# One PSUM tile of four banks split into four one-bank tiles, with a new order for the first pair's cycle

## The chip, the cores and the metric

The kernel runs on one core of one Trainium2 chip. The metric is the device time of the whole program in microseconds, the median of several executions. One execution was taken with the hardware profiler; its rows are used below.

## The reference

The program is a clustered attention followed by two feed-forward blocks, all in fp32.

```python
q_assign = argmax(einsum('bhsd,hcd->bhsc', q_n, c_n))     # nearest of 16 centroids, also for k
mask = q_assign[:, :, :, None] == k_assign[:, :, None, :]
scores = where(mask, scale * q @ k.T, -1e9)
attn = softmax(scores);  x = attn @ v                       # (2, 8, 768, 64) -> (1536, 512)
h = x @ w_in;   x = (h * cos(h)) @ w_out                    # d_ff 2048
h = x @ w_in2;  out = blend(h) @ w_out2                     # 0, (h+1)^2/4 or h
```

Batch is 2, there are 8 heads, 768 positions and 64 elements per head. The weights arrive as 64-bit floats and are converted on the chip.

## The kernel before, in words

The two heads of a "pair" are worked on together; there are 8 pairs (2 batches by 4 pairs of heads). Each pair is one cycle of the attention, and after the cycles come the two feed-forward blocks, which are long rows of matmuls on TensorE (PE). Every engine takes its instructions strictly in the order in which the program issues them.

That order is written out by hand as a string of words, which `run_cycle` (line 719) reads. `BEGIN` (790) is the cycle of pair 0, `CYCLE` (793) that of pairs 1 to 5, `LATE` (796) and `LAST` (799) those of pairs 6 and 7, `END` (802) the rest. A letter is a step, a digit its part, and a prime moves it to the pair before. Cycle c does these steps:

- S0 to S11: scores of one block of 128 rows (four matmuls, lines 583 and 586, into a two-bank tile of a pool of two) and its row maximum on VectorE (DVE, 593). S0 to S5 are the first head, S6 to S11 the second.
- E0 to E11: the exponential on ScalarE (ACT, 601, with the read of its sum). A pool of two score tiles means that S(n) waits for E(n-2).
- G0 to G11: three transposes of the first head's probabilities on PE (644) into a bank that `bank3()` hands out, and a copy of the bank on ACT (646). V0 to V5: probabilities times v (651), accumulated in bank 3. X: that sum times the inverse row sums, on DVE (656).
- T6 to T11: the second head's probabilities, transposed on DVE (677). W0 to W3: 192 small matmuls (686) into all four banks, the "strips". Z: the sum of the strips (`x_sum`, 692): ACT copies partitions 64 to 127 of all four banks (696), then DVE adds partitions 0 to 63 (697).
- Q0 to Q3, D, C, m, t, n, O, H, J: the preparation of the pairs to come. Q transposes q and k (491), ACT copies the bank (497), GpSimd (POOL) splits it (499, 500); D and C are products with the centroids, there and back (510, 512, 518); m and n (527, 528, 537, 538) are DVE steps that read C's bank; O transposes the one-hot rows (545, 547); H and J are DMAs (473).
- R and B: inverse row sums (608 to 617) and their spread by DMA (625, 630). L, v, r: loads of q and k (235), v (243), v of the second head (254). w: one step of the conversion of a weight chunk (157 to 176).

All DMAs of the attention are issued by one queue, SP, in the order of the words.

The PSUM is eight banks of 512 fp32 per partition. Four belong to the score tiles. The other four are one tile, `big` (line 212). `bank3()` (215) hands out its banks 0, 1 and 2 in turn; bank 3 holds V's sum, and in the first pair's preparation (`first_pair`, 291) matmuls without use (297) that keep PE busy. The framework puts in all waits between engines: an instruction waits for earlier ones of other engines that touched the same tile, by its own record of tiles.

Of the kernel before, what the change touches and what calls it, by code (L numbers as in the profile page):

```python
# [9 lines left out]
F32 = mybir.dt.float32  # L10
# [4 lines left out]
AF = mybir.ActivationFunctionType  # L15
ALU = mybir.AluOpType
# [3 lines left out]
P = 128  # L20
# [13 lines left out]
def attention_moe_moe(  # L34
# [18 lines left out]
    nc = tc.nc  # L53
    B, H, S, D = q.shape
    C = centroids.shape[1]
    NT, DM = out.shape
    DFF = w1_in.shape[1]
    NJ = S // P
    HJ = NJ // 2
    HS = S // 2  # L60
# [147 lines left out]
    with ExitStack() as actx:  # L208
        ap = actx.enter_context(tc.tile_pool(name="apool", bufs=1))
        ps_s = []  # L210
        ps_b = actx.enter_context(tc.tile_pool(name="ps_b", bufs=1, space=PSUM))
        big = ps_b.tile([P, 4, 512], F32, name="big")
        turn_of = [0]

        def bank3():
            turn_of[0] += 1
            return big[:, turn_of[0] % 3, :HS]

        idle = ap.tile([P, HS], F32, tag="pt", bufs=PT_BUFS, name="idle").bitcast(BF16)[:, :512]
        nc.vector.memset(idle, 0.0)  # L220
# [3 lines left out]
        nat, v_of, vr_of = {}, {}, {}  # L224
# [65 lines left out]

        def first_pair():

            idle_o = big[:, 3]

            def run_idle(n):
                for _ in range(n):
# [20 lines left out]
            t = nat.pop(0)  # L317
# [19 lines left out]
            def put(dst, src):  # L337
                return nc.sync.dma_start(dst.bitcast(F32), src.bitcast(F32))

            pc = bank3()[:, :P]  # L340
            turn(0, 0)
            turn(0, 1)
# [17 lines left out]
            for hf in range(2):  # L360
                nc.scalar.activation(th[:, 1, cols(hf)], qk[1, hf], AF.Copy)
                nc.vector.tensor_tensor(tl[:, 1, cols(hf)], qk[1, hf],
                                        th[:, 1, cols(hf)].bitcast(F32), ALU.subtract)

            dt = bank3()
            cw = cn32[:, 0].rearrange("p h c -> p (h c)")
            for hf in range(2):
# [46 lines left out]
            def turn_rows(h, s, pars=(0, 1)):  # L414
                po = bank3().rearrange("p (j n) -> p j n", n=P)
                for jp in range(HJ):
                    rows = dotv[h][:, s, 2 * jp:2 * jp + 2].rearrange("p r h c -> p (r h c)")
                    rows = rows[:, pars[0] * 2 * C:(pars[-1] + 1) * 2 * C]
                    nc.tensor.transpose(po[:2 * C * len(pars), jp], rows, ident)
                return {par: po[n * 2 * C:(n + 1) * 2 * C] for n, par in enumerate(pars)}  # L420
# [227 lines left out]

        def p_v(i, kt):
            for hf in range(2):  # L650
                nc.tensor.matmul(big[hf * D:(hf + 1) * D, 3, :HS], v_of[i][:, kt],  # L651
                                 pts.pop((i, 2 * kt + hf)), start=kt == 0, stop=kt == NJ - 1)

        def x_rows(i):
            x = rb[2 * i]
            nc.vector.tensor_tensor(x, big[:, 3, :HS], x, ALU.mult)

        def x_parts(i):
            x32 = rb.pop(2 * i)
# [19 lines left out]
        def p_v_square(i, n, parts):  # L679
            t, vr = sq[i], vr_of[i]  # L680
            for cp in range(12 * n // parts, 12 * (n + 1) // parts):
                for a in range(4):
                    rows = slice(32 * a, 32 * a + 32)
                    for par in range(2):
                        kt, g = divmod(2 * cp + par, 4)
                        nc.tensor.matmul(  # L686
                            big[par * D:(par + 1) * D, a, :NJ * 32],
                            vr[rows, g, kt * D:(kt + 1) * D],
                            t[rows, 2 * cp + par].rearrange("p j r -> p (j r)"),
                            start=cp == 0, stop=cp == 11, tile_position=(32 * a, par * D))  # L690

        def x_sum(i):
            x = xpool.tile([P, S], F32, tag="xs", bufs=1, name=f"xs{i}")
            xv = x[D:].rearrange("p (j a r) -> p a j r", j=NJ, r=32)
            o = big[:, :, :NJ * 32].rearrange("p a (j r) -> p a j r", r=32)
            nc.scalar.activation(xv, o[D:], AF.Copy)
            nc.vector.tensor_tensor(xv, o[:D], xv, ALU.add)
            xs[i] = x[D:]

        def x_out(i):  # L700
# [18 lines left out]
        def run_cycle(c, order):  # L719
# [4 lines left out]
            for word in words:  # L724
# [18 lines left out]
                elif what == "G":  # L743
                    p_transpose(i, arg)
                elif what == "V":
                    p_v(i, arg)
                elif what == "X":
                    x_rows(i)
                elif what == "Y":
                    x_parts(i)  # L750
                elif what == "R":
                    inverse(2 * i + arg)
                elif what == "B":
                    spread(2 * i + arg)
                elif what == "W":
                    p_v_square(i, arg, parts)
                elif what == "Z":
                    x_sum(i)
                elif what == "z":
                    x_out(i)  # L760
# [26 lines left out]
                elif what == "w":  # L787
                    pump(arg or 1)

        BEGIN = ("L' S3 m' E3 S4 t' S5 E4 H0' n' G0 E5 R0 O' G1 G2 S6 G3 G4 J0' E6 S7 G5 r T6 V0 E7 H1' V1 G6 "  # L790
                 "G7 S8 T7 B0 Q0 J1' E8 G8 G9 Q1 V2 S9 T8 G10 G11 Q2 Q3 L S10 E9 E10 T9 V3 D S11 E11 C m V4 t "
                 "n ")
        CYCLE = ("Q0 S0 Q1 S1 H0' E0 Q2 E1 T10' O' V5' S2 Q3 S3 E2 E3 J0' D T11' X' G0 S4 E4 v' S5 W0' W1' R1' "
                 "J1' E5 R0 W2' W3' Y' L Z' S6 S7 G1 B1' G2 G3 E6 C G4 E7 V0 H1' m V1 T6 T7 G5 G6 t G7 S8 n G8 "
                 "r G9 G10 E8 S9 B0 T8 V2 E9 V3 S10 G11 S11 E10 T9 E11 z' V4 ")
# [5 lines left out]
                 "S10 G11 w S11 E10 T9 E11 z' V4 ")  # L801
        END = ("T10' V5' T11' X' R1' W0' B1' W1' W2' W3' Z' Y' z' ")
        first_pair()
        for c in range(NP):
            run_cycle(c, {0: BEGIN, 6: LATE, 7: LAST}.get(c, CYCLE))
        run_cycle(NP, END)
# [8 lines left out]
    while len(wslot) < 2:  # L815
        n = len(wslot)
# [148 lines left out]
```

## Time and profile before

| | us |
|---|---|
| median of 3 executions | 940.75 (928.43 to 942.93) |
| the profiled execution, whole | 924.13 |
| its span, first to last instruction | 922.3 |
| PE busy in the span | 808.5 (88%) |
| DVE busy | 587.6 (64%) |
| ACT busy | 365.1 (40%) |
| POOL busy | 254.4 (28%) |
| mean granted PE clock, share of full speed | 0.913 |

The times of rows are counted from the span's start. Busy time of PE counts the modelled ends of matmuls that follow one another in a pipeline, so that two neighbours overlap in the sum. In a row of the timeline, the brackets give how long the engine sat idle before the instruction and what ended the wait.

### The profile page before, as it was taken

The numbers are of one execution on the slowest core, as the hardware profiler recorded it, in microseconds if no ns is written. First come the engines' busy times: TensorE is split into PE (matmuls) and PEld (weight loads), VectorE is DVE, ScalarE is ACT, GpSimd is POOL, SyncE is SP. The second block draws the span as 40 slices with busy tenths as digits, with TensorE's granted clock in tenths as the row PEclk, the third lists the DMA queues.
The fourth block names the chain that finished last, engine by engine and source line by source line (L and its number), as shares of the span: only waits on it lengthen the run. The fifth ranks groups of instructions, "written<-read, shape, count | busy, mean of one in ns | idle before, by whom it ended". The sixth has DMA issues, their size and how long they took to land.

```text
span 922.3 us, 12700 instructions
## 1 busy us (share of the span) xinstructions
PE 808.5 (88%) x4957; PEld 619.6 (67%) x4957; DVE 587.6 (64%) x805; ACT 365.1 (40%) x650; POOL 254.4 (28%) x374
## 2 busy tenths in 40 slices
PE   7677777767777777849999999999999999999998
PEld 4445454545454544638888888888888888888887
DVE  4425453653446574688777878888888687764543
ACT  3534353563454454345443344343225433222220
POOL 5123433443242223443222212123332112211110
PEclk8659696997599788979999999999999999999999
DMA  7524635372437422222122212121121221100012
GB/s 172 133 64 93 142 68 140 71 178 72 104 93 173 105 65 53 101 91 91 57 85 90 87 50 92 47 92 45 47 92 47 92 83 54 46 1 1 0 46 92
DMA packets 52621, 74.97 MB, mean 81 GB/s; under 512 B 28977, under 2 KB 36369, under 8 KB 52561
## 3 DMA queue, kind: packets, MB, share of 16 engines
q1 hardware_dynamic: 52272, 73.99, 29.0%
q8 instruction: 39, 0.64, 0.3%
q14 instruction: 22, 0.17, 0.1%
q10 hardware_dynamic: 288, 0.16, 0.1%
HBM read 50.89 MB, written 3.19 MB: 59 GB/s over the span
## 4 chain that ended last, share of the span: by engine, by line
PE 78%; ACT 6%; DVE 6%; issue 4%; DMA 3%; POOL 2%; SPq 1%; ACTq 0%; DVEq 0%; POOLq 0%
PE y L859 9%; PE y L861 9%; PE y L860 9%; PE h L859 9%; PE h L860 9%; PE h L861 9%; PE big L644 6%; PE big L651 4%; PE s L583 3%; PE s L586 3%; PE big L686 3%; ACT p_t L646 3%; DMA st<-tt 2%; DVE nm L593 2%; SPq L473 1%
## 5 line engine op out<-in xcount | busy, mean ns | idle before, releaser
L593 DVE TENSOR_REDUCE nm<-s 128x1 f32<-128x768 f32 x96 | 90.7, 955 | 119.7 <-PE s L586 118.7
L859 PE MATMUL h<-xh,w 128*128 128x512 f32 x384 | 151.2, 394 | 15.1 <-DVE g L838 12.2
L860 PE MATMUL h<-xl,w 128*128 128x512 f32 x384 | 150.7, 393 | 0.0
L861 PE MATMUL h<-xh,w 128*128 128x512 f32 x384 | 150.6, 392 | 0.0
L821 POOL TENSOR_SCALAR gh<-g 128x512 fp32r<-128x512 f32 x96 | 73.4, 765 | 278.8 <-DVE g L852 159.8
L644 PE MATMUL big<-ident,p 128*128 128x128 f32 x288 | 65.2, 347 | 49.7 <-ACT p_t L646 29.3
L601 ACT ACTIVATE p<-s,nm 128x768 f32<-128x768 f32 x96 | 86.3, 899 | 33.9 <-DVE nm L593 31.6
L644 PEld LDWEIGHTS big<-ident,p 128*128 128x128 f32 x288 | 39.2, 171 | 81.8 <-ACT p_t L646 45.0
L859 PEld LDWEIGHTS h<-xh,w 128*128 128x128 f32 x384 | 73.0, 190 | 31.5 <-DVE g L838 12.9
L646 ACT ACTIVATE p_t<-big 128x384 f32<-128x384 f32 x96 | 47.1, 490 | 108.5 <-PE big L644 107.9
L825 DVE TENSOR_TENSOR gl<-g,gh 128x512 fp32r<-128x512 f32 x96 | 74.5, 776 | 21.8 <-POOL gh L821 15.8
L583 PE MATMUL s<-st,st 128*128 128x384 f32 x192 | 82.5, 429 | 3.7 <-ACT p L601 3.4
L848 ACT ACTIVATE p<-h,ones 128x512 f32<-128x512 f32 x48 | 33.0, 688 | 133.0 <-DVE m L847 132.6
L860 PEld LDWEIGHTS h<-xl,w 128*128 128x128 f32 x384 | 73.1, 190 | 15.4 <-issue 0.3
L861 PEld LDWEIGHTS h<-xh,w 128*128 128x128 f32 x384 | 72.8, 190 | 15.3
L157 ACT ACTIVATE wx<-wraw 128x1024 f32<-128x1024 f32 x32 | 36.1, 1129 | 104.9 <-DVE w L176 46.1
L586 PE MATMUL s<-st,st 80*128 80x384 f32 (+1 forms) x192 | 73.6, 383 | 1.9 <-DVE st L429 1.9
L859 PE MATMUL y<-gh,w 128*128 128x512 f32 x192 | 74.7, 389 | 0.0
L860 PE MATMUL y<-gl,w 128*128 128x512 f32 x192 | 74.7, 389 | 0.0
L861 PE MATMUL y<-gh,w 128*128 128x512 f32 x192 | 74.7, 389 | 0.0
L861 PE MATMUL y<-w,gl 128*128 128x512 f32 (+1 forms) x192 | 74.3, 387 | 0.0
L860 PE MATMUL y<-w,gh 128*128 128x512 f32 (+1 forms) x192 | 74.3, 387 | 0.0
(138 smaller groups left out, 1419.5 us busy)
## 6 DMA issues: line engine op xcount, KB each, us to landing
wraw<-in_moe_w_in_dram SPq DMA_DIRECT2D x16, 1024.0 KB
wraw<-in_moe_w_out_dram SPq DMA_DIRECT2D x16, 1024.0 KB
st<-tt SPq DMA_DIRECT2D x63, 192.0 KB
st<-tt SPq DMA_DIRECT2D x16, 384.0 KB
vr<-in_v_dram SPq DMA_DIRECT2D x32, 192.0 KB
nat<-in_q_dram SPq DMA_DIRECT2D x8, 384.0 KB
nat<-in_k_dram SPq DMA_DIRECT2D x8, 384.0 KB
out_dram<-acc SPq DMA_DIRECT2D x11, 256.0 KB
```

Of the source, the lines that this page charges most:

```text
L583: nc.tensor.matmul(s[:, step, :HS], qt[:, 0, cols], kt[:, 0, kc], start=True, stop=False)
L586: nc.tensor.matmul(s[:, step, :HS], qt[:rows, 1, cols], kt[:rows, 1, kc], start=False, stop=True)
L593: nc.vector.tensor_reduce(nm, s[:, :, :HS], AX.XY, ALU.max, negate=True)
L601: nc.scalar.activation(p.rearrange("p (a n) -> p a n", a=2), s[:, :, :HS], AF.Exp, bias=nm, accum_out=dens[d][:, jj:jj + 1])
L644: nc.tensor.transpose(ps[:, jj * P:(jj + 1) * P], p[:, kt * P:(kt + 1) * P], ident)
L646: nc.scalar.activation(pt, ps, AF.Copy)
L651: nc.tensor.matmul(big[hf * D:(hf + 1) * D, 3, :HS], v_of[i][:, kt], pts.pop((i, 2 * kt + hf)), start=kt == 0, stop=kt == NJ - 1)
L821: nc.gpsimd.tensor_scalar(hi, g, 1.0, 0.0, ALU.mult, ALU.add)
L825: nc.vector.tensor_tensor(lo, g, hi.bitcast(F32), ALU.subtract)
L859: nc.tensor.matmul(o, lh, rh, start=first, stop=False)
L860: nc.tensor.matmul(o, lh, rl, start=False, stop=False)
L861: nc.tensor.matmul(o, ll, rh, start=False, stop=last)
```

## The change

Four tiles of one bank each take the place of the one tile of four. Everything that used a bank of `big` uses a tile now. The turn of `bank3()` begins with bank 0 in place of bank 1. The sum of the strips is made in four steps of one bank, each an ACT copy and a DVE add of 192 columns (64 partitions), where it was one copy and one add of 768 columns. `BEGIN` holds the same words in another order: the transposes G0, G2 and G4, which need the first three blocks alone, come before the scores of the blocks after them, and Q0 to Q3 come earlier.

```diff
-        big = ps_b.tile([P, 4, 512], F32, name="big")
-        turn_of = [0]
+        big = [ps_b.tile([P, 512], F32, name=f"big{n}") for n in range(4)]
+        turn_of = [2]
 
         def bank3():
             turn_of[0] += 1
-            return big[:, turn_of[0] % 3, :HS]
+            return big[turn_of[0] % 3][:, :HS]
...
-            idle_o = big[:, 3]
+            idle_o = big[3]
...
-                nc.tensor.matmul(big[hf * D:(hf + 1) * D, 3, :HS], v_of[i][:, kt],
+                nc.tensor.matmul(big[3][hf * D:(hf + 1) * D, :HS], v_of[i][:, kt],
...
-            nc.vector.tensor_tensor(x, big[:, 3, :HS], x, ALU.mult)
+            nc.vector.tensor_tensor(x, big[3][:, :HS], x, ALU.mult)
...
-                            big[par * D:(par + 1) * D, a, :NJ * 32],
+                            big[a][par * D:(par + 1) * D, :NJ * 32],
...
             xv = x[D:].rearrange("p (j a r) -> p a j r", j=NJ, r=32)
-            o = big[:, :, :NJ * 32].rearrange("p a (j r) -> p a j r", r=32)
-            nc.scalar.activation(xv, o[D:], AF.Copy)
-            nc.vector.tensor_tensor(xv, o[:D], xv, ALU.add)
+            for a in range(4):
+                o = big[a][:, :NJ * 32].rearrange("p (j r) -> p j r", r=32)
+                nc.scalar.activation(xv[:, a], o[D:], AF.Copy)
+                nc.vector.tensor_tensor(xv[:, a], o[:D], xv[:, a], ALU.add)
...
-        BEGIN = ("L' S3 m' E3 S4 t' S5 E4 H0' n' G0 E5 R0 O' G1 G2 S6 G3 G4 J0' E6 S7 G5 r T6 V0 E7 H1' V1 G6 "
-                 "G7 S8 T7 B0 Q0 J1' E8 G8 G9 Q1 V2 S9 T8 G10 G11 Q2 Q3 L S10 E9 E10 T9 V3 D S11 E11 C m V4 t "
-                 "n ")
+        BEGIN = ("L' S3 G0 m' E3 t' G2 S4 G4 E4 n' S5 H0' E5 Q0 O' G1 Q1 G3 S6 V0 Q2 Q3 L J0' E6 G5 G6 S7 T6 V1 E7 G7 H1' G8 S8 T7 E8 G9 G10 S9 V2 T8 J1' E9 R0 r G11 D S10 V3 E10 T9 C m B0 S11 E11 V4 t n ")
```

## Rows read from the trace of the kernel before

**Rows 1.** Stretch, length, busy PE, PEld, DVE, ACT, POOL, PE clock, DMA share, GB/s.
```profile
30.10:75.00 44.90, 33.25 (x116) 20.22 (x115) 15.70 (x22) 17.38 (x36) 8.47 (x14) 0.54 0.38 90
75.00:118.80 43.80, 33.41 (x328) 21.59 (x326) 21.13 (x31) 19.54 (x40) 17.00 (x26) 0.81 0.44 102
...
202.20:252.00 49.80, 38.91 (x329) 25.64 (x327) 21.38 (x31) 20.67 (x44) 16.59 (x25) 0.69 0.40 97
252.00:291.00 39.00, 28.07 (x328) 18.83 (x326) 22.38 (x32) 20.91 (x45) 16.59 (x25) 1.00 0.54 129
291.00:331.20 40.20, 29.71 (x304) 20.50 (x305) 23.25 (x31) 19.67 (x40) 10.67 (x17) 0.83 0.51 126
331.20:372.10 40.90, 31.05 (x302) 20.86 (x304) 24.27 (x32) 18.92 (x37) 10.32 (x17) 0.79 0.21 60
372.10:405.20 33.10, 18.01 (x246) 13.93 (x242) 22.53 (x27) 9.40 (x15) 13.11 (x15) 0.81 0.21 70
405.20:922.30 517.10, 513.87 (x2268) 425.62 (x2268) 381.26 (x507) 183.74 (x287) 115.42 (x136) 1.00 0.18 62
```

**Rows 2.** Timeline of PE in the sixth cycle: start, length, instruction, idle time before it.
```profile
263.52 0.55 PE L644 MATMUL big<-ident,p 128*128 128x128 f32 x3 [2.25 <-DVE rb L656]
...
265.41 4.49 PE L686 MATMUL big<-ptb,vr 32*64 32x192 f32 x192
...
272.97 0.55 PE L644 MATMUL big<-ident,p 128*128 128x128 f32 x3 [0.58 <-ACT p_t L646]
...
278.87 0.87 PE L651 MATMUL big<-p_t,v 128*64 128x384 f32 x4 [1.33 <-DVE both L528]
...
288.88 0.49 PE L644 MATMUL big<-ident,p 128*128 128x128 f32 x3
289.13 0.42 PE L583 MATMUL s<-st,st 128*128 128x384 f32 x1
...
290.00 0.87 PE L651 MATMUL big<-p_t,v 128*64 128x384 f32 x4
```

**Rows 3.** Waits of the whole run: who waited for whom, total us, times, longest.
```profile
PE big L644 <- ACT p_t L646: 29.3, 49, 0.6
...
DVE mx L527 <- PE big L651: 23.2, 5, 5.7
...
PE big L644 <- DVE rb L656: 16.2, 7, 2.5
...
PE big L518 <- DVE st L433: 2.5, 1, 2.5
```

**Rows 4.** Timeline of ACT in the sixth cycle.
```profile
254.35 0.49 ACT L497 ACTIVATE t<-big 128x384 f32<-128x384 f32 x1 [0.70 <-POOL tt L499]
```

**Rows 5.** Groups by line: engine, instruction, count, busy us, mean ns, idle before.
```profile
L601 ACT ACTIVATE p<-s,nm 128x768 f32<-128x768 f32 x96 | 86.3, 899 | 33.9 <-DVE nm L593 31.6 <-DVE den L608 1.4
...
L646 ACT ACTIVATE p_t<-big 128x384 f32<-128x384 f32 x96 | 47.1, 490 | 108.5 <-PE big L644 107.9
...
L601 ACT ACTIVATION_READ_ACCUMULATOR p<-s,nm 128x1 f32 x96 | 18.9, 197 | 0.0
...
L697 DVE TENSOR_TENSOR xs<-big,xs 64x768 f32<-64x768 f32 x8 | 7.6, 952 | 17.8 <-ACT xs L696 17.8
...
L696 ACT ACTIVATE xs<-big 64x768 f32<-64x768 f32 x8 | 6.5, 807 | 18.9 <-PE big L686 18.8
...
L547 ACT ACTIVATE oht<-big,ohbias,ohscale 128x384 fp32r<-128x384 f32 x7 | 4.7, 666 | 1.1 <-PE big L545 1.1
L656 DVE TENSOR_TENSOR rb<-big,rb 128x384 f32<-128x384 f32 x8 | 4.3, 541 | 2.8 <-ACT both L512 2.8
```

**Rows 6.** Timeline of the SP queue in the third cycle: first and last of 12 rows.
```profile
118.13 4.55 SPq L473 DMA_DIRECT2D st<-tt  x5
...
150.27 1.11 SPq L630 DMA_DIRECT2D rb<-flat  x2
```

**Rows 7.** Busy time of the third cycle's long burst of loads, columns as in rows 1.
```profile
141.00:154.00 13.00, 8.74 (x32) 4.56 (x30) 4.07 (x6) 4.71 (x10) 5.86 (x5) 0.59 0.98 237
```

## The prediction

> **What bounds the kernel now.** I read the busy time by stretch first [rows 1]. After 405.2 us PE is busy in practically all of the 517.1 us left, at a granted clock of 1.00 (2.4 GHz): the feed-forward blocks are bound by PE's matmuls, and the change doesn't touch them. Before that lies the attention: about 30 us of preparation, BEGIN with 44.9 us, five CYCLEs with 216 us together (75.0 to 291.0), LATE and LAST with 40.2 and 40.9, and a transition of 33.1. In a CYCLE no engine is full: ACT and DVE each work 20 to 22 us of 39 to 50. So it is bound by waits between engines.
>
> The timeline of PE shows which ones [rows 2]. A group of three transposes takes PE 0.25 us when nothing stops it (288.88, next instruction 289.13). But G2 at 272.97 sat until ACT had copied the bank of the group before, though it writes another bank; G0 at 263.52 waited 2.25 us for X, a DVE read of bank 3 that G0 doesn't touch; V1 at 278.87, which writes bank 3, waited 1.33 us for DVE's step m, which reads C's bank. The list of waits [rows 3] has the same over the whole run: 29.3 us of transposes behind copies, 16.2 us behind X, and in the other direction 23.2 us of m behind V. Each of these pairs shares no bank, only the tile `big`. Whoever comes next to the tile waits for whoever came before, so three banks in turn serve as one buffer.
>
> **The cycle without these waits.** I take the sixth cycle (252.0 to 291.0), which ran at full clock. By the order string, 14 PE steps of a CYCLE wait for another bank's reader: Q1, O, V5, G0, G1, G2, G3, C, V0, V1, G6, G7, G9, G10. With a tile per bank the true waits are left: a bank is free when the copy three turns back is done, V needs its own copies, S(n) needs E(n-2). I go through the words with the durations of the rows.
>
> First part, from Q0 (251.98) to W (265.41), 13.4 us. The next late thing is ACT, which has its copies and exponentials in one order. Q1's copy starts at 254.35, 2.4 us after Q0; its wait there is for POOL [rows 4], which I leave. Behind it ACT has Q2, Q3, D and G0 to copy (with Q1 five of 0.49), O (0.67) and E0 to E3 (0.90 and 0.20 each) [rows 5]: 2.45 + 0.67 + 4.40 = 7.5. W needs G0's bank copied, so it starts at 2.4 + 7.5 = 9.9 in place of 13.4: 3.5 less. PE's own work there hides beside it: by [rows 2] a group of transposes is 0.25, an S 0.87 (289.13 to 290.00), a V 0.87, and with D taken like V that is 6 x 0.25 + 6 x 0.87 + 2 x 0.87 = 8.5.
>
> W itself, 4.4 us of PE to the next S, stays.
>
> Second part, from W's end (269.8) to the next Q0 (291.0), 21.2 us, with ten of the 14 waits. ACT has there Z, eleven copies of 0.49 and E6 to E9, before the last V4: 1.3 + 5.4 + 4.4 = 11.1. PE has six S, eleven G, C and five V: 5.2 + 3.0 + 4.4 = 12.6. Neither can start all of it at once (G1 behind Z, S10 behind E8, V2 behind G5's copy), but the S figure holds a little slack, so I take 13.0: 8.2 less. The cycle is then 39.0 - 3.5 - 8.2 = 27.3 us. ACT's whole work is 12 x 1.10 + 17 x 0.49 + 0.67 + 1.3 = 23.5, which no order can go below.
>
> **The sum of the strips.** From two rows of ACT on PSUM [rows 5], 807 ns for 768 columns and 490 for 384, one of 192 columns takes 490 - 159 = 331 ns; for DVE, 952 and 541, it is 335. Whether a copy of the second bank can run beside the add of the first, the trace doesn't show, for both write interleaved columns of one SBUF tile. If they overlap, Z takes 4 x 0.33 + 0.34 = 1.7 us, against 0.81 + 0.95 = 1.8 before; if each hands over to the other, 4 x (0.33 + 0.34) and seven handovers of 0.04 (G2's idle 0.58 holds a copy of 0.49 and two of them), 3.0. Behind it in ACT's queue stand G1's copy and E6, in DVE's the maxima of S6 and S7. G1 itself gets its bank earlier either way, after 0.7 to 2.0 us. I take 0.6 more per cycle, and in all for Z and what the two queues below may add, 29.0 in place of 27.3 us per CYCLE.
>
> The Trainium skill, Perfetto Trace Analysis, section Optimizing Scalar/DVE Operations, speaks against the split: each ScalarE or DVE instruction pays a data-access overhead, which larger operations spread. The rows agree that there is one: they give 0.17 us of an ACT copy that doesn't go with its columns, so three more copies cost 0.5 us; by the page's about 51 ns on PSUM, seen twice as long in a profile, an estimate would be 0.3. The sum changes by under 2 us over eight cycles.
>
> **What lies beside.** SP issues a CYCLE's DMAs in 23.2 us (12 rows, first and last in [rows 6]), in order; at 29 us it is 80% full. The long burst of loads runs 13 us at 237 GB/s and 0.98 of the DMA engines [rows 7]. A CYCLE moves 97 GB/s x 49.8 us = 4.8 MB, so 20 us of such a rate. Both still fit, with little room: q and k for the next Q0 are issued behind R0's DMA.
>
> **BEGIN, LATE, LAST, the preparation.** BEGIN has nine E, twelve G, four Q, O and D on ACT: 9.9 + 17 x 0.49 + 0.67 = 18.9 us. In the new order G0, G2 and G4 come before they can be held up by later scores, E8 stands before G9 and G10 (whose banks are then free without it), and R0 moves back behind E9, some 5 us before X needs it in the next cycle, enough for POOL's line and two DMAs. With the CYCLE's ratio (29.0 / 23.5) BEGIN is 23.3; it begins with PE at half clock (0.54 in [rows 1]) and loads for Q0 that are issued shortly before, so I take 27.5, 17.4 less. What the new order alone is worth can't be read; I bound it from 0 to 8 us of these. LATE and LAST have the conversion of weights on DVE: 24.3 us busy in LAST [rows 1], the most of any engine. I take 29.5 each, 22.1 less together. The preparation holds a few such waits, one of 2.5 us [rows 3]; I take 2.5, bounds 0 and 4. The transition stays: PE is busy for 18.0 of its 33.1 us and DVE for 22.5 [rows 1], the conversion of the first weights among it, none of which touches `big`.
>
> **The sum.** 2.5 + 17.4 + (216 - 5 x 29.0 = 71.0) + 22.1 = 113 us. From the profiled 924.1 that is 811. The profiled run lies 16.6 below the median shown; cycles at 0.69 and 1.00 of clock took 49.8 and 39.0 [rows 1], so the spread of the runs is probably such cycles, which a denser PE should have less of. I add 4: **815 us**.
>
> The Trainium skill, PSUM — Partial Sum Buffer, section PSUM bank collisions raise a hardware error, asks for semaphores between engines per bank and quadrant of partitions, and says that different banks run clean. The waits of [rows 3] between banks are thus more than the chip asks; if that page is right nothing else makes them come back, and the sum stands as it is.
>
> **Rivals.**
> *SP and the loads become the bound.* With ACT's waits gone, SP is 80% full, and each of its waits (for O's copy, for R's line) is idle time that it can't make up. For: [rows 6, 7]. Against: its waits lie mostly where nothing is due. Then CYCLEs are 34, LATE and LAST too, BEGIN 32: gain 2.5 + 12.9 + 46 + 13.1 = 74.5, time 850.
> *The PE clock stays low.* From [rows 1], 0.31 of clock cost 10.8 us; at 0.81, as in the second cycle, 29 becomes 35.6, BEGIN 39: gain 6 + 38 + 10 = 54, time 870. Against: two cycles with all these stalls ran at 1.00, so fewer stalls should do no worse.
> *Slower: the waits stay and Z is longer.* If the framework's record follows something other than the tile (the pool, or PSUM as a whole), the 14 waits remain and the four steps of Z hand over one by one, 1.2 us more in each of eight cycles: 924 + 10 = 934, and about 950 on the median. It decides if none of the 14 goes; one that goes (0.8 us) nearly pays for it. Against: the score tiles and those of the feed-forward blocks are separate tiles, and PE there doesn't stand behind each reader (513.9 of 517.1 us busy, [rows 1]).
>
> **Chances.** The forecast (795 to 833) 0.64, SP or loads (833 to 858) 0.22, clock (858 to 900) 0.10, waits stay 0.04. If the replay's 27.3 holds everywhere and BEGIN is 24, the gain is 127 and the time 797: the low end. The range 795 to 857 leaves out some 0.18. A measurement of this kernel tells about 2% from no change, here 19 us. Faster by more than that: 0.96; within: 0.03; slower: 0.01, the last rival at its worst.
>
> **What would show it.** Right: in the list of waits, transposes behind ACT's copies fall from 29.3 us to a few, and G behind X and m behind V vanish; CYCLEs between 27 and 31 us, with PE's clock near 1.00 and ACT over 75% busy; W some 10 us after Q0. The step is wrong where G2 and G3 still stand 1.1 us apart, where ACT sits idle behind DVE through Z, or where Q0 waits for a load. Under 795 the replay was too careful; over 857 another queue has taken over.

## The result and the profile after

The kernel after takes **781.57 us**, the median of 4 executions (779.75 to 782.67), against 936.62 of 4 of the kernel before (928.43 to 942.93): a ratio of 0.837, 95% interval 0.829 to 0.844. The direction was right. The forecast of 815 was 33 us too slow, and its range (795 to 857) lay wholly above the result.

The profiled execution took 781.32 us (span 779.5), 142.8 less than that of before. The stages first, as in [rows 1]. A cycle runs from its first Q or S on PE to the next one's.

Busy time by stretch of the kernel after: preparation, BEGIN, first, third and fourth CYCLE, LATE, LAST, transition, feed-forward blocks. Columns as in [rows 1].
```profile
0.00:18.98 18.98, 16.27 (x93) 10.00 (x95) 11.31 (x37) 11.14 (x23) 12.33 (x51) 1.00 0.87 200
18.98:42.31 23.33, 21.33 (x121) 14.22 (x118) 16.46 (x24) 16.93 (x38) 8.65 (x14) 0.93 0.76 170
42.31:70.70 28.39, 26.31 (x328) 19.23 (x326) 22.30 (x36) 19.58 (x46) 15.76 (x25) 1.00 0.72 175
97.55:123.48 25.93, 25.74 (x329) 19.26 (x327) 21.20 (x34) 20.04 (x47) 17.63 (x26) 1.00 0.82 194
123.48:148.86 25.38, 25.38 (x329) 19.14 (x327) 21.21 (x34) 20.05 (x47) 15.27 (x25) 1.00 0.76 176
175.20:202.60 27.40, 25.26 (x305) 18.44 (x304) 23.11 (x34) 19.16 (x44) 9.81 (x17) 0.94 0.74 173
202.60:229.10 26.50, 24.01 (x304) 17.37 (x304) 23.91 (x36) 18.35 (x41) 12.94 (x18) 1.00 0.40 129
229.10:262.37 33.27, 16.30 (x243) 12.76 (x241) 21.29 (x29) 9.41 (x16) 15.51 (x16) 0.85 0.22 76
262.37:779.50 517.13, 513.74 (x2268) 425.32 (x2268) 381.59 (x507) 182.96 (x287) 111.83 (x136) 1.00 0.18 62
```

Lengths in us:

| stage | before | forecast | after |
|---|---|---|---|
| preparation (to the first S of BEGIN) | 29.5 | 27.0 | 19.0 |
| BEGIN | 45.5 | 27.5 | 23.3 |
| five CYCLEs | 216 | 145 | 132.9 |
| LATE and LAST | 81.1 | 59.0 | 53.9 |
| transition and feed-forward | 550.2 | 550.2 | 550.4 |

Each stage of the attention is shorter than forecast; the last line is the same to 0.2 us. The four differences are 8, 4, 12 and 5 us; with the 4 added for the median they make the miss. (Each cycle is counted here from its first instruction on PE; the prediction took BEGIN from 30.1, 44.9 us.)

The timeline of the kernel after, in order of time: PE in the preparation, then PE, ACT and DVE in the third CYCLE (97.55 to 123.48).
```profile
9.68 1.15 PE L491 MATMUL big<-ident,nat 128*128 128x128 f32 x9
...
97.55 0.55 PE L491 MATMUL big<-ident,nat 128*128 128x128 f32 x3
...
98.74 1.01 ACT L497 ACTIVATE t<-big 128x384 f32<-128x384 f32 x2
...
103.96 0.66 PE L644 MATMUL big<-ident,p 128*128 128x128 f32 x3
...
105.54 0.49 ACT L646 ACTIVATE p_t<-big 128x384 f32<-128x384 f32 x1
...
106.22 3.95 PE L686 MATMUL big<-ptb,vr 32*64 32x192 f32 x177
110.36 0.58 PE L686 MATMUL big<-ptb,vr 32*64 32x192 f32 x15 [0.19 <-issue]
110.87 0.44 PE L583 MATMUL s<-st,st 128*128 128x384 f32 x1
...
110.99 0.98 ACT L697 ACTIVATE xs<-big 64x192 f32<-64x192 f32 x4 [2.60 <-PE big L686]
...
111.35 1.15 DVE L698 TENSOR_TENSOR xs<-big,xs 64x192 f32<-64x192 f32 x4 [2.15 <-ACT xs L697]
...
112.39 1.15 PE L644 MATMUL big<-ident,p 128*128 128x128 f32 x9
...
112.91 1.26 ACT L646 ACTIVATE p_t<-big 128x384 f32<-128x384 f32 x3 [0.94 <-PE big L644]
...
123.48 0.55 PE L491 MATMUL big<-ident,nat 128*128 128x128 f32 x3
```
Where G2 stood behind the copy of the group before [rows 2], G1, G2 and G3 now run as one piece of nine transposes in 1.15 us (112.39). G0 has no wait for X (103.96). The strips' sum takes 1.5 us (110.99 to 112.50) with copies and adds overlapping. In the 25.9 us of this cycle PE has one gap that the timeline marks: 0.19 us.

The groups of PE by line, from 97 to 202 us of the kernel after: instructions, busy us, mean ns, idle time before them.
```profile
L583 PE MATMUL s<-st,st 128*128 128x384 f32 x96 | 36.9, 384 | 1.3 <-ACT p L601 1.1
...
L644 PE MATMUL big<-ident,p 128*128 128x128 f32 x144 | 20.8, 278 | 0.8 <-ACT p L601 0.8
...
L686 PE MATMUL big<-ptb,vr 32*64 32x192 f32 x768 | 18.6, 339 | 0.6 <-issue 0.6
```
All of PE's idle time in these 105 us is 2.7. By these rows a cycle that was bound by waits is now nearly all PE's own work; as the ends of PE's matmuls are modelled, the runs below test it.

The waits of the whole run of the kernel after, columns as in [rows 3].
```profile
DVE nm L593 <- PE s L586: 16.5, 31, 3.3
PEld s L583 <- ACT p L601: 16.5, 26, 1.6
...
PE h L858 <- DVE g L837: 15.2, 2, 15.0
```
The four lines of [rows 3] are gone; DVE's maxima wait 16.5 us for scores and PE's weight loads 16.5 for exponentials, little of which stops PE in the CYCLEs (2.7 above). The longest single wait of PE is one of 15.0 us, in the transition.

### The profile page after: what moved, and what is told of

It reads as the page before. It is cut to its first block, busy times and chain, and to the rows that moved or that the text cites. A ratio compares the mean times of both kernels' runs of the same rounds, so it can differ in the third digit from the quotient of the medians.

```text
span 779.5 us, 12769 instructions
## 1 busy us (share of the span) xinstructions
PE 746.2 (96%) x4956; PEld 594.4 (76%) x4957; DVE 585.0 (75%) x829; ACT 357.5 (46%) x674; POOL 254.4 (33%) x374
## 4 chain that ended last, share of the span: by engine, by line
PE 87%; DVE 5%; POOL 2%; issue 2%; DMA 2%; ACT 1%; SPq 0%; POOLq 0%; DVEq 0%; ACTq 0%
PE y L859 11%; PE y L858 11%; PE y L860 11%; PE h L858 11%; PE h L859 10%; PE h L860 10%; PE s L583 4%; PE big L651 4%; PE big L644 4%; PE big L686 3%; PE s L586 3%; DVE nm L593 1%; PE big L491 1%; DMA wraw<-in_moe_w_out_dram 1%; ACT p L601 1%
## 5 line engine op out<-in xcount | busy, mean ns | idle before, releaser
L820 POOL TENSOR_SCALAR gh<-g 128x512 fp32r<-128x512 f32 x96 | 70.1, 730 | 280.7 <-DVE g L851 159.0
L593 DVE TENSOR_REDUCE nm<-s 128x1 f32<-128x768 f32 x96 | 90.3, 951 | 18.2 <-PE s L586 16.5
L583 PE MATMUL s<-st,st 128*128 128x384 f32 x192 | 74.0, 385 | 5.9 <-ACT p L601 4.5
L859 PE MATMUL y<-w,gh 128*128 128x512 f32 (+1 forms) x192 | 74.3, 387 | 0.0
L858 PE MATMUL y<-w,gh 128*128 128x512 f32 (+1 forms) x192 | 74.3, 387 | 0.0
L913 DVE TENSOR_TENSOR acc<-y,acc 128x512 f32<-128x512 f32 x71 | 48.3, 684 | 30.4 <-PE y L860 30.4
L173 POOL TENSOR_SCALAR w<-wx 128x1024 fp32r<-128x1024 f32 x32 | 34.6, 1082 | 102.8 <-DVE wx L167 101.0
L586 PE MATMUL s<-st,st 80*128 80x384 f32 (+1 forms) x192 | 65.7, 342 | 0.0
```

The costliest lines, as they stand in the source:

```text
L173: nc.gpsimd.tensor_scalar(hi, x, 1.0, 0.0, ALU.mult, ALU.add)
L583: nc.tensor.matmul(s[:, step, :HS], qt[:, 0, cols], kt[:, 0, kc], start=True, stop=False)
L586: nc.tensor.matmul(s[:, step, :HS], qt[:rows, 1, cols], kt[:rows, 1, kc], start=False, stop=True)
L593: nc.vector.tensor_reduce(nm, s[:, :, :HS], AX.XY, ALU.max, negate=True)
L820: nc.gpsimd.tensor_scalar(hi, g, 1.0, 0.0, ALU.mult, ALU.add)
L858: nc.tensor.matmul(o, lh, rh, start=first, stop=False)
```

## The experiments

Each kernel was timed beside the kernel before on its own chip. Ratios are to that.

**Which part of the change does it?** The kernel after with the BEGIN of before:
```diff
-        BEGIN = ("L' S3 G0 m' E3 t' G2 S4 G4 E4 n' ...
+        BEGIN = ("L' S3 m' E3 S4 t' S5 E4 H0' n' G0 ...
```


> Four one-bank tiles, with the old order of the first pair's cycle. Theory (the waits between banks carry the gain, the new order 0 to 8 us of it): 782 to 790 us, the first cycle 23 to 31 us long. Rival (the new order carries the 22 us that the first cycle lost): the first cycle stays near 40 us and the whole is at 798 or above.


Measured 781.07 (778.87 to 783.99), ratio 0.834 (0.828 to 0.840): the new order is worth nothing that can be measured. The profile shows why. The first CYCLE's Q0 starts at 47.12 in place of 42.31, after 2.30 us of waiting for its load, so the new order does save 4.8 us there. At LATE's W 2.8 of them are left (187.65 against 184.86), at the last V 1.9 (229.61 against 227.69), and PE's first long stretch of the feed-forward blocks starts at 262.17 against 262.37, for PE waits 13.31 us ahead of it for DVE, so its own lead is lost there (the transition, below). The new start of `bank3()`'s turn is in every kernel here with parted banks and wasn't tried by itself.

The kernel before with the sum in four steps:
```diff
-            o = big[:, :, :NJ * 32].rearrange("p a (j r) -> p a j r", r=32)
-            nc.scalar.activation(xv, o[D:], AF.Copy)
-            nc.vector.tensor_tensor(xv, o[:D], xv, ALU.add)
+            for a in range(4):
+                o = big[:, a, :NJ * 32].rearrange("p (j r) -> p j r", r=32)
+                nc.scalar.activation(xv[:, a], o[D:], AF.Copy)
+                nc.vector.tensor_tensor(xv[:, a], o[:D], xv[:, a], ALU.add)
```


> The kernel before, one tile of four banks, with only the sum of the strips made in four steps. Theory (the steps alone free nothing, as the tile is still one record): 925 to 950 us; if the copies and adds hand over to one another inside the one tile, the sum takes about 3 us in place of 1.8 and each cycle grows by 0.5 to 1.2 us. Rival (making the sum bank by bank is itself a gain, as the first bank comes free early): below 925 us.


Measured 959.46 (957.17 to 962.29), ratio 1.024 (1.016 to 1.033): the steps alone free nothing, as expected, but the loss is larger than the range allowed. Its timeline, ACT, DVE and PE in one cycle:
```profile
286.17 0.33 ACT L697 ACTIVATE xs<-big 64x192 f32<-64x192 f32 x1 [3.64 <-PE big L686]
286.52 0.35 DVE L698 TENSOR_TENSOR xs<-big,xs 64x192 f32<-64x192 f32 x1 [3.19 <-ACT xs L697]
286.91 0.33 ACT L697 ACTIVATE xs<-big 64x192 f32<-64x192 f32 x1 [0.42 <-DVE xs L698]
...
289.16 0.55 PE L644 MATMUL big<-ident,p 128*128 128x128 f32 x3 [1.57 <-DVE xs L698]
```
With one tile each copy stands behind the add of the bank before: 2.9 us (286.17 to 289.10), where the handover bound of the prediction said 3.0, and G1 waits 1.57 us. With four tiles the same eight instructions take 1.5. So it was the record of `big` that made them alternate, and not the SBUF tile that both write. The longer sum makes about 1.1 us a cycle, some 9 of the 20 us or more that were lost. The rest fits the lower clock (0.873 on average in the profiled run, and 0.69 to 0.75 in its five CYCLEs, where [rows 1] has 0.69 to 1.00); no run separates the two.

The kernel before with bank 3 a tile of its own and banks 0 to 2 one tile (and the sum by bank):
```diff
-        big = ps_b.tile([P, 4, 512], F32, name="big")
+        big3 = ps_b.tile([P, 3, 512], F32, name="bigt")
+        big = [big3[:, n] for n in range(3)] + [ps_b.tile([P, 512], F32, name="bigv")]
```


> Banks 0 to 2 are one tile, bank 3 is another; sum by bank, old order of the first cycle. Five of the 14 waits of a cycle go (V5, G0 behind X, V0, V1 behind m, and m behind V), nine stay (transposes behind the copy of the bank before). Theory (the waits add up): about 45% of the gain, 850 to 880 us. Rival (the three banks as one buffer are the whole matter, bank 3 hides nothing): above 900 us.


Measured 876.91 (876.72 to 877.11), ratio 0.936 (0.926 to 0.946): 62 us, some 40% of the whole gain. Against the kernel with the sum by bank alone (959.46) it is 83 us; what bank 3 apart is worth without that sum wasn't run. The waits of [rows 3] show where it comes from: G behind X and m behind V are no longer in the list, the transposes behind the copies are there as before, 49 times. From the list of waits of that kernel:
```profile
PE bigt L645 <- ACT p_t L647: 29.6, 49, 0.9
...
DVE mx L528 <- ACT p_t L647: 16.1, 5, 3.8
```
Step m, which reads C's bank, now waits for copies of other banks of the tile of three. The other 60% of the whole gain came only when these three were parted too (781.07 above, with the same order of the first cycle).

**Is it the number of banks?** The kernel after with two banks in turn:
```diff
-            return big[turn_of[0] % 3][:, :HS]
+            return big[turn_of[0] % 2][:, :HS]
```


> The kernel after, with the working tiles turning over two banks in place of three; the fourth stays with the scores' own tile as before. If what the tile of four banks cost was that a writer had to wait for readers of other banks, two nearly do: 785 to 800 us. If a third bank is needed to hide the copies' latency (a step is written, copied and the one after that written): 820 or more, since each of some ten steps a cycle would wait 0.4 to 0.6 us again.


(The fourth bank is V's, not the scores'.) Measured 799.23 (798.12 to 800.33), ratio 0.856 (0.848 to 0.864): at the upper end of the first answer. Most of the gain needs two banks that are free of each other; the third is worth 17.7 us. PE in one cycle of that kernel, one of four such waits of 0.20 to 0.31 us, which are for the copy two turns back:
```profile
125.44 0.55 PE L644 MATMUL big<-ident,p 128*128 128x128 f32 x3 [0.31 <-ACT p_t L646]
```

**The preparation by itself.** The kernel after, with one tile of four banks up to C of the first pair, in a pool that is then closed:
```diff
-        big = [ps_b.tile([P, 512], F32, name=f"big{n}") for n in range(4)]
+        bigp = pool_p.tile([P, 4, 512], F32, name="bigp")
+        big = [bigp[:, n] for n in range(4)]
...
+            ps_p.close()
+            big[:] = [ps_b.tile([P, 512], F32, name=f"big{n}") for n in range(4)]
             one.back()
```


> The changed kernel, but the first pair's preparation uses one tile of four banks as before; the four tiles come in at its end. Theory (the preparation's own waits between banks were worth 8 to 10 us, more than the 2.5 forecast): 789 to 793 us, and the first scores start at 19 to 22 us in place of 14.6. Rival (the preparation got faster for another cause, the clock or the loads): 781 to 784 us.


Measured 790.90 (787.92 to 794.76), ratio 0.845 (0.838 to 0.851): 9.3 us more than after. In its profile the first scores start at 18.07 (14.64 after), a little before the 19 to 22 expected, and BEGIN's first at 28.52 (18.98 after). So the preparation's own waits are worth 9, where the prediction took 2.5 with bounds of 0 and 4. They could have been read: here is PE in the preparation of the kernel before.
```profile
8.79 0.85 PE L370 MATMUL big<-t,cn 128*32 128x384 f32 x8 [0.72 <-ACT tt L361]
...
10.76 0.55 PE L380 MATMUL pd<-ident,both 128*128 128x128 f32 x3 [0.58 <-ACT both L377]
...
12.29 0.55 PE L491 MATMUL big<-ident,nat 128*128 128x128 f32 x3 [0.66 <-ACT t L497]
13.48 0.89 PE L491 MATMUL big<-ident,nat 128*128 128x128 f32 x3 [0.64 <-ACT t L497]
15.01 1.86 PE L297 MATMUL big<-idle 128*128 128x512 bf16 x4 [0.64 <-ACT t L497]
...
21.85 0.41 PE L586 MATMUL s<-st,st 96*128 96x384 f32 x1 [1.88 <-DVE st L429]
...
25.14 0.84 PE L419 MATMUL big<-ident,dots 128*64 128x128 f32 x6 [0.69 <-ACT both L512]
...
29.22 0.52 PE L518 MATMUL big<-ident,both 128*128 128x128 f32 x3 [2.53 <-DVE st L433]
```
These eight are 8.3 us. Two of them (`pd`, `s`) don't touch `big` themselves; all eight are back in the run with one tile, at 0.58 to 2.53 us, and in the kernel after PE has two waits in this stretch, of 0.47 and 0.91. Q's nine transposes, three times three here with waits between, are there one piece of 1.15 us (9.68 above). Of the eight only the last stood out in the list of waits, where each line of the code has an entry of its own.

**What sets the cycle now?** Three kernels give one engine or queue more to do. On ACT, four more copies per cycle:
```diff
+            if g in (2, 5, 8, 10):
+                nc.scalar.activation(pt, pt, AF.Copy)
```


> The kernel after, with four more copies of 128 columns in place on ScalarE per cycle, about 0.42 us each by the back-to-back copies of the profile after. If ScalarE sets the cycle's length, most of 1.7 us is added eight times: 791 to 797 us. If ScalarE has slack there: under 785.


Measured 785.35 (785.09 to 785.61), ratio 0.841 (0.833 to 0.848). (The copies have 384 columns each, not 128.) Of some 13 us of ACT work 3.8 came through, just over the "under 785" of the second answer and far from the first: ACT has slack behind W, where these copies stand. Ahead of W no run adds to it.

On PE, at the same places:
```diff
-            for jj in range(HJ):
+            for jj in [*range(HJ)] * (3 if g in (2, 5, 8, 10) else 1):
```


> The kernel after, with the three transposes of G2, G5, G8 and G10 written three times over in place of once: six more of about 0.083 us, 0.5 us of TensorE each time, 2.0 us a cycle, at the same four places where the other kernel has more copies on ScalarE. If TensorE sets the cycle's length now (its steps add up to 25.5 of 26.6 us), nearly all comes through eight times: 794 to 799 us. If the chains between the engines set it, a part is taken up by TensorE's waits: 782 to 788.


Measured 802.99 (802.40 to 803.58), ratio 0.861 (0.853 to 0.869). All 16 us came through and 5.4 more: above the range of either answer, but far on PE's side. The third CYCLE took 27.97 us against 25.93, the 2.0 that were added, with no idle time of PE. From LATE's W to LAST's it is 33.2 against 27.0; that stretch has a granted clock of 0.85 and one wait of 2.62 us at a score block, and most of the excess lies there.

On SP, four more small DMAs per pair, which nothing waits for (the expectation calls them loads; they write `ident` to DRAM):
```diff
+                if h == 0:
+                    for n in range(4):
+                        nc.sync.dma_start(more[32 * n:32 * n + 32], ident[32 * n:32 * n + 32])
```


> The kernel after, with four more loads on SP's queue per cycle that nothing waits for, about 0.6 us of issue each, 2.5 us a cycle. SP issues for 23.2 of a cycle's 26.6 us. If SP has the slack that these numbers say (3.4 us), at most 2 us are added in all: up to 784. If SP is already a limit of the cycle (the loads' rival of the prediction), 1 to 2.5 us are added to each of five cycles: 787 to 794.


Measured 794.70 (793.55 to 795.84), ratio 0.851 (0.843 to 0.859): 13.1 us, at the second answer's upper edge (794). The SP queue of that kernel, from one v load to the next:
```profile
117.83 0.38 SPq L243 DMA_DIRECT2D v<-in_v_dram  x1
118.31 0.28 SPq L621 DMA_DIRECT2D flat<-line  x1
...
141.94 2.99 SPq L568 DMA_DIRECT2D more<-ident  x4
145.03 0.36 SPq L243 DMA_DIRECT2D v<-in_v_dram  x1
```
It runs with hardly a gap, 27.2 us a round. The second to fourth CYCLE take 27.5, 26.7 and 27.2 us, 0.7 to 1.8 more than after, and the first 32.5, 4.1 more. The DMA engines' share in the third and fourth is 0.76 and 0.74, no higher than after (0.82 and 0.76), so the engines are no fuller for it. In the kernel after, a round from the load of v at 107.59 to the next at 132.09 has 22.8 us of issue in 24.5. So SP's slack is far smaller than 3.4 us: PE sets the cycle of the kernel after, and SP stands right behind it. How a late SP reaches PE, in one cycle of the run with more DMAs:
```profile
120.42 1.03 POOL L618 TENSOR_SCALAR line<-turned 6x32 f32<-6x32 f32 x4 [4.35 <-DMA flat<-line]
...
126.40 0.55 DVE L537 TENSOR_REDUCE mx<-both 128x24 f32<-128x384 f32 x1 [0.75 <-POOL both L533]
...
128.51 0.90 ACT L605 ACTIVATE p<-s,nm 128x768 f32<-128x768 f32 x1 [1.29 <-DVE nm L597]
...
129.55 0.45 PE L587 MATMUL s<-st,st 128*128 128x384 f32 x1 [0.53 <-ACT p L605]
```
The write of the inverse row sums (`flat`, 118.31) goes out behind the added DMAs, and POOL can't write the next line before it has landed (4.35 us of wait; 1.42 at the same place in the third CYCLE of after). POOL is then late with step t, DVE with n (which reads t's result, not C's bank) and with the maximum of S9 behind it, ACT with E9, and PE's S11 waits for E9.

Less work on PE, by leaving out half of the strips' products (the second head's result lacks half of its keys):
```diff
-            for cp in range(12 * n // parts, 12 * (n + 1) // parts):
+            for cp in range(6 * n // parts, 6 * (n + 1) // parts):
```


> The kernel after with half of the strips' matmuls left out (96 of 192 per pair; the second head's result lacks half of its keys), some 2.0 us of TensorE less in each of nine places. If TensorE sets the cycle's length, eight cycles lose 1.6 to 2.0 us each: 764 to 769 us. If SP's queue, which issues for 23.2 us a cycle, stands right behind, CYCLEs stop at about 25.5: 771 to 776.


Measured 764.33 (763.75 to 764.92), ratio 0.820 (0.812 to 0.827). The time is that of the first answer, the profile is not. The second to fourth CYCLE took 24.6, 24.5 and 24.7 us in place of 26.9, 25.9 and 25.4, and the W of END starts at 226.56 against 232.95: 6.4 us from the seven W ahead of it, where 11 to 14 were expected (the expectation counted eight cycles; the first has no W). The rest is gained behind, some 2.4 us in END's own W and what stands around it, and 7.0 in PE's long wait of the transition, 7.99 in place of 14.98. By its time alone the run would have passed as proof. In the third and fourth CYCLE PE has idle time again, 0.46 and 1.03 us at S11 behind the chain shown above. But SP issues the write of the line only 0.2 and 0.3 us after POOL has made it, so here that chain with its DMA stands next to PE, and that SP's queue is what holds the CYCLEs near 24.6 isn't shown.

**The transition.** The kernel after with S6 and E6 moved into W, where ACT idles for 2.60 us (110.99 above), in CYCLE, LATE and LAST:
```diff
-   ... E5 R0 W2' W3' Y' L Z' S6 S7 G1 B1' G2 G3 E6 C G4 ...
+   ... E5 R0 S6 W2' E6 W3' Y' L Z' S7 G1 B1' G2 G3 C G4 ...
```


> The kernel after, with the sixth score step S6 put ahead of W2' and its exponentials E6 ahead of W3' in CYCLE, LATE and LAST, where ScalarE stands idle for some 2.6 us of a cycle. If ScalarE's order is what sets a cycle's length now, 0.5 to 1.1 us go per cycle, eight times: 772 to 778 us. If TensorE or SP's queue sets it, nothing goes: 780 to 784, or a little more because W's steps come later. I expect the first with a chance of a half.


Measured 776.70 (775.79 to 780.01), ratio 0.832 (0.826 to 0.839). The time fits ACT's order as the bound, but the first four CYCLEs took 108.1 us together against 106.6 of after: nothing was gained there. The order by hand ends behind END; the framework orders the feed-forward blocks itself, and with another LAST it orders them otherwise. So the same edit in LAST alone was run:


> The kernel after, with S6 and E6 moved into W in LAST alone. The framework orders the feed-forward blocks by itself, and with this LAST it puts the third weight chunk's first step behind four other steps on ScalarE at the start of these blocks, as it did in the kernel that moved S6 in all cycles; there TensorE's wait at that place was 8.0 us in place of 15.0. If that is where that kernel's 5 us came from, they are here too: 775 to 778 us. If they came from the cycles, nothing is left: 780 to 783.


Measured 776.20 (775.71 to 777.11), ratio 0.833 (0.827 to 0.838). All of the gain is there. ACT, then PE, at the start of the feed-forward blocks, in the kernel after:
```profile
255.77 1.15 ACT L157 ACTIVATE wx<-wraw 128x1024 f32<-128x1024 f32 x1 [7.66 <-DMA wraw<-in_moe_w_in_dram]
...
258.23 0.63 ACT L833 ACTIVATE r<-r 128x512 f32<-128x512 f32 x1
...
262.37 0.80 PE L858 MATMUL h<-xh,w 128*128 128x512 f32 x1 [14.98 <-DVE g L837]
```
and with S6 moved in LAST:
```profile
253.70 0.63 ACT L831 ACTIVATE r<-r 128x512 f32<-128x512 f32 x1 [5.37 <-DVE r L830]
...
255.23 1.12 ACT L157 ACTIVATE wx<-wraw 128x1024 f32<-128x1024 f32 x1
...
256.19 0.79 PE L856 MATMUL h<-xh,w 128*128 128x512 f32 x1 [7.76 <-DVE g L835]
```
In the first the cosine's step (258.23, and 253.70 in the second) stands on ACT behind a step that waits 7.66 us for a load of weights; in the second that step comes behind it (255.23). This kernel beats the kernel after: its four times lie below all four of after (779.75 to 782.67), by 0.7% at the medians, though the two were not timed side by side.

## Why the prediction was wrong, and where it was right

*What bounds the kernel* held: the waits of [rows 3] belong to the tile and not to the banks, and go with it. The sum by bank shows it alone: in one tile its eight instructions go one by one, though they touch different banks, in four tiles they overlap. The rival in which the waits stay fell with this. The Trainium skill's PSUM — Partial Sum Buffer, section PSUM bank collisions raise a hardware error, says that different banks run clean; the trace agrees (nine transposes in 1.15 us while ACT copies).

*The step that failed: the sizes of the sum, first of all "29.0 in place of 27.3 us per CYCLE".* The mechanism was right and the gain was put too low, in several terms. This surcharge, for Z and what the two queues might add, is 8.5 of the 12 us over the five CYCLEs and wasn't due. Z took 1.5 us (110.99 to 112.50), under the lower bound of 1.7, and stands beside PE's S6 and S7; and in 97 to 202 us PE sat idle for 2.7 us in all, so the queues added next to nothing.

*The step "The next late thing is ACT"* makes the other 3.6. The prediction had 9.9 us for the first part, from ACT, 4.4 for W, and 13.0 for the second, from PE's 12.6. The third CYCLE's three parts took 8.7, 4.65 and 12.6 (97.55, 106.22, 110.87, 123.48), the fourth cycle 25.4 in all. These are PE's sums, 8.5 and 4.4 and 12.6 = 25.5, which stand in the prediction and were set aside in the first part. ACT's 9.9 was too long twice over. It held a wait "for POOL, which I leave" [rows 4]. After the change Q0's and Q1's copies run back to back (98.74) with POOL's steps as long as before: the copy of Q1 had waited for its own transposes, which stood behind Q0's copy, so this was one more wait of the kind that goes. The row's releaser was taken for the cause. And durations of single rows were added up although neighbours on ACT overlap: from Q1's copy to the end of G0's at 106.03, ACT took 6.8 us in place of 7.5. The 23.5 us "which no order can go below" has the same fault: [rows 1] shows ACT busy for 20.91 in that very cycle, and the kernel after for 20.04. Still, in the first part PE isn't alone: G0's copy ends only 0.19 us before W starts, so ACT has hardly any slack there.

*The preparation, "I take 2.5, bounds 0 and 4"*, was mis-sized as badly, 8 of the 33 us: 10.5 in the profile, 9.3 by the experiment. One wait was counted and eight were there, so the bounds were no bounds.

*BEGIN* came out at 23.3 us, just what the CYCLE's ratio gave. That is luck in part, as the ratio holds the surcharge; the 4.2 us added for a PE at half clock and late loads weren't due, for the clock was 0.93 there. *LATE and LAST* took the CYCLE's error with them, 5 us. That the new order brings 0 to 8 us of BEGIN's held at BEGIN's end (4.8) and at 0 for the whole. *The 4 us for the median* weren't needed: the profiled run lies 0.25 us from the median.

*The rivals.* SP didn't take over, yet it came closer than "80% full" says: 22.8 us of issue in a round of 24.5, with the run with four more DMAs to show that little room is left. The low clock went the other way: the mean granted clock rose from 0.913 to 0.987, and where CYCLEs of before show 0.69 and 0.81 [rows 1], all five of after show 1.00. Two of the CYCLEs of before ran at 1.00, the one that the prediction replayed and this one (columns as in [rows 1]):
```profile
163.10:202.20 39.10, 28.26 (x329) 18.94 (x327) 21.34 (x31) 20.76 (x44) 16.56 (x25) 1.00 0.52 122
```
Had all five taken the 39 us of these two, they would have been 195 us, so by that some 21 of their 83 us of gain came with the clock; the prediction had them, as it replayed such a cycle. BEGIN's clock rose too, from 0.54 to 0.93, and what of its 22 us came with that isn't split off.

*The transition* stayed as said, but not only for the reason given, the work of PE and DVE: part of it is an order on ACT that the framework chose, and 5 us of it can be had.

## What to carry to other kernels

Where a wait goes, add up every engine's own work for the stage, from its busy time and not from single rows, and take the largest as the new length; a chain that comes out above it by a microsecond needs each of its waits questioned, for some go with the same edit. Sum up all waits of the kind in every stage, not only those that a list by line puts on top. Several buffers in one tile are one buffer to whoever waits by tile, so give each PSUM bank that turns over a tile of its own. A small gain in the time isn't yet a proof of its reason: two runs here had the time that was expected of them, from another place.

## What was not expected of the hardware

Neighbouring copies on ACT overlap in part. Three copies of 384 columns take 1.26 us (112.91), 0.42 each, where one by itself takes 0.49 [rows 5]; four of 192 columns take 0.98 (110.99), 0.17 more than the one of 768 columns with its 807 ns. So each further copy cost 0.06 us, a third of the 0.17 that the prediction worked out from single rows. The Trainium skill's Perfetto Trace Analysis, section Optimizing Scalar/DVE Operations, gives about 51 ns of access overhead for a ScalarE operation on PSUM, and says that a profile shows about twice that, of which half overlaps with the next instruction. The trace agrees with the 51 ns, at 0.06 us for each further copy. The prediction's estimate of 0.3 us from that page counted the doubled figure, where three more copies took 0.17.
